# Windowed attention beside a Mish feed-forward on one core: kept rest chunks in a padded layout, one transfer for each rest tile, and another table of places

## The chip, the cores and the metric

The kernel runs on one core of a Trainium2 chip. The metric is the device time of one execution in microseconds (us); lower is better. Three runs of the kernel before took 1120.54, 1127.26 and 1128.27 us, so its median is 1127.26 us.

## What is computed

The input `x` has 2048 rows of 576 columns. Each row is normalised; the result goes through two branches, and both are added to `x`:

```python
xn = (x - mean) / sqrt(var + eps)
# A: 32 heads of 18 columns; a row sees itself and the 7 rows 2, 4, ... 14 before it
q, k, v = split(xn @ wqkv)                       # 576 x 1728
attn = softmax(q . k[pos - 2 * (0..7)] * scale)  # masked where pos - 2 w < 0
A = (attn . v[pos - 2 * (0..7)]) @ wo            # 576 x 576
# B: dense, Mish, dense
h = xn @ w1 + b1                                 # 576 x 4608
B = (h * tanh(softplus(h))) @ w2                 # 4608 x 576
out = x + A + B
```

## The kernel before

**Tiling.** The rows are worked on in two halves (`hf`) of 1024. A product in fp32 is made from numbers split into a high and a low part, so that one tile product costs three matmuls (high x high, high x low, low x high). Most products use a scheme of seven block products for a 2 x 2 block product; the blocks of the weights are called B11, B21, B22 and the sums T1 to T4, those of the activations A11 to A22 and S1 to S4.

**The rest.** The contraction of 576 is four tiles of 128 rows and a rest of 64 rows, 32 for each block row. For the rest, high and low parts are put side by side on the 128 partitions, so that one matmul does the three products of a block. The rest rows of the weights come in as `in_wqr` (for the queries, keys and values) and `in_w1r` (for `w1`). They are prepared in chunks: `c_load` (L1149) brings a chunk in, `c_sum` (L1154, GpSimd) forms the T sums, `c_high` (L1157, ScalarE) and `c_low` (L1161, VectorE) split it, and `c_keep` (L1169) writes it to a tensor in HBM, `ckept`. Chunks "0" and "y" are done whole; "1" to "4" and "v" are done in four pieces of a quarter of their columns each: 32 of 128 columns for "1" to "4", 27 of 108 for "v".

**Reading them back.** `wr_fetch` (L1177) reads the tile `wr` for one step `q` of the feed-forward from `ckept`: 128 partitions of 7 blocks of 128 columns, in two transfers of 64 partitions that read the same rows. `rest_fetch` (L1190) reads the tiles `rest_y`, `rest_v` and `rest_z` for the query, key and value products, also in two transfers each. `wr` has 36 tiles in all, and they share two buffers with some of the rest tiles.

**The order of the work.** The program is a plan of 451 slots. Each slot holds one item of TensorE work (M): a part of a first dense product (`h`, L1388), a group of a second dense product (`po`, L1489, L1579, L1601), a piece of the query, key and value products (`y`, `v`, `z`, L1060) or of the output product (`o`, L1766). All other work is cut into 3316 small functions ("atoms"): loads, splits, evictions, attention steps, stores. The table `PLACES` names for each slot the atoms in their order, and M where its matmuls stand. The instructions of each engine then run in the order in which the atoms were written. `PLACES` thus sets the order on VectorE (DVE), ScalarE (ACT), GpSimd (POOL) and on SyncE (SP), which issues every transfer of the kernel. SP takes its transfers strictly one after the other, and hands them to eight semaphores in turn; a transfer waits until the one before it on its semaphore has landed, until its buffer is free, and until its data are there.

Transfers that the prediction speaks of: `t` (T sums of `w1`: t0, t1), `wa` and `wc` (blocks of `w1`), `wr`, all for the first product; `pw` (blocks of `w2` for the second); `kv` and `q` (attention's inputs); `o_d` (attention's output, stored); `vw_*` and `z_*` (weights of the v and z products); `kv_d`, `q_d` (their results, stored). In a name such as `t1_1_3` the last two numbers are the half and the step `q`. Evictions: L1493 (DVE) adds a `po` result to `acc` and so frees a buffer that a later `po` group writes.

Of the kernel before, what the change touches and what calls it, by code (L numbers as in the profile page):

```python
# [9 lines left out]
F32 = mybir.dt.float32  # L10
# [8 lines left out]
P = 128  # L19
# [14 lines left out]
RB = 32  # L34
CP = 4
QC = UQ * CU * 3 // 4

# [248 lines left out]
PLACES = ("b2 p33 b0 b1 b3 b6 b8 b4 b7 b9 b5 b11 b12 b13 M", "b10 m0a m0b b14 b16 b7a b15 M",  # L286
# [222 lines left out]
def block_kernel(ctx: ExitStack, tc: tile.TileContext, x, wq, wqd, wqr, wo, w1, w1r, b1, w2, mask, sign, out):  # L509
# [620 lines left out]
    def c_tiles(c):  # L1130
        return 7, QC if c[0] in "yv" else P, 64 if c[0] == "4" else P

# [30 lines left out]
    def c_keep(c):  # L1163
        lo, hi, cols = chunk[c]
        n, w, rows = c_tiles(c)
        if c[0] not in ckept:
            ckept[c[0]] = dram.tile([2, rows, n, w], F32, name=f"ckept_{c[0]}")
        for h, t in ((0, hi.bitcast(F32)), (1, lo)):
            nc.sync.dma_start(ckept[c[0]][h][:, :, cols], t)  # L1169
# [1214 lines left out]
```

## Time and profile before

| | |
|---|---|
| time of the profiled execution | 1120.96 us |
| its span, first to last instruction | 1119.2 us |
| mean granted TensorE clock | 0.991 |
| TensorE busy | 1089.2 us, 97% of the span |
| VectorE / ScalarE / GpSimd busy | 899.0 / 522.0 / 801.3 us |
| moved by DMA | 297.15 MB in 241954 packets, 266 GB/s over the span |

The page of the profile gives such sums for one execution. TensorE (PE) is busy nearly all the time, so what matters is where it is not: the timeline of PE gives, in brackets behind a row, how long PE sat idle before that row and what ended the wait. The view by stretches gives busy time of each engine, the granted clock of TensorE (PEclk, 1.00 is full speed), the mean share of the 16 DMA engines that were busy, and the rate in GB/s, for any stretch of the span. The timeline of SP (SPq) shows when each transfer was issued; a long row there means that issues were held up. The list of transfers gives for each kind the count, KB each and the median time from issue to landing.

### The profile page before, as it was taken

The page shows a single profiled execution, that of the slowest core. Times are in us where ns is not written, and L with a number is a line of the kernel's source. Part 1 is how long each engine was busy: PE and PEld are TensorE (multiplying, and loading weights), DVE is VectorE, ACT ScalarE, POOL GpSimd, SP SyncE. Part 2 cuts the span into 40 slices and gives each one's busy share as a digit, 9 for nine tenths or more (in the row PEclk, how much of TensorE's full clock was granted, in tenths as well). Part 3 has the DMA queues.
Part 4 walks back from the last instruction along what each step waited for, and adds up shares of the span by engine and source line. Part 5 has one row for each costly group of instructions (what it writes and reads, how often), then busy time and mean ns, then how long its engine had stood idle before and what let it go on. Part 6 is the DMA issues. An engine that isn't in the chain of part 4 may idle for free.

```text
span 1119.2 us, 18531 instructions
## 1 busy us (share of the span) xinstructions
PE 1089.2 (97%) x6420; PEld 998.4 (89%) x6420; DVE 899.0 (80%) x1520; ACT 522.0 (47%) x994; POOL 801.3 (72%) x709
## 2 busy tenths in 40 slices
PE   8999999999999999989998999999999999999998
PEld 8889899999998898879988878999999898999998
DVE  6897887897888889868996475888788786678886
ACT  7655553654554444547622253524344424343353
POOL 3474888796877688957897488687777687968532
PEclk9999999999999999999999998999999999999999
DMA  7899999879888789996999999678687768697864
GB/s 265 275 292 313 343 307 297 269 247 318 291 258 266 215 251 313 273 279 197 296 337 286 303 291 332 219 251 277 218 257 230 222 198 249 179 316 246 299 185 163
DMA packets 241954, 297.15 MB, mean 266 GB/s; under 512 B 101666, under 2 KB 177860, under 8 KB 241860
## 3 DMA queue, kind: packets, MB, share of 16 engines
q1 hardware_dynamic: 241860, 295.96, 84.9%
q8 instruction: 51, 0.84, 0.3%
q14 instruction: 43, 0.35, 0.1%
HBM read 180.51 MB, written 115.38 MB: 264 GB/s over the span
## 4 chain that ended last, share of the span: by engine, by line
PE 72%; DMA 9%; DVE 6%; POOL 3%; issue 2%; SPq 2%; ACT 1%; DVEq 0%; POOLq 0%; ACTq 0%
PE h L1388 29%; PE po L1489 17%; PE po L1579 11%; PE po L1601 6%; PE o L1766 5%; DMA wr<-ckept 2%; PE v L1060 1%; DMA rw<-in_w 1%; POOL pr L1244 1%; POOL pv L1283 1%; DVE L L1249 1%; DVE acc L1493 1%; DMA vw_B<-kept_wq 1%; DMA z_T<-kept_yT 1%; DMA vw_T<-kept_vT 1%
## 5 line engine op out<-in xcount | busy, mean ns | idle before, releaser
L1489 PE MATMUL po<-w,act 128*128 128x288 f32 x1728 | 244.1, 297 | 3.7 <-DVE acc L1493 3.3
L1489 PEld LDWEIGHTS po<-w,act 128*128 128x128 f32 x1728 | 237.7, 189 | 11.2 <-DVE acc L1493 5.2
L1283 POOL TENSOR_TENSOR pv<-L,kv 128x576 f32<-128x576 f32 x128 | 172.7, 1457 | 56.8 <-DVE L L1276 24.2
L1244 POOL TENSOR_TENSOR pr<-q,kv 128x576 f32<-128x576 f32 x128 | 193.0, 1538 | 9.4 <-DVE og L1289 3.7
L1493 DVE TENSOR_TENSOR acc<-po,acc 128x288 f32<-128x288 f32 x288 | 119.9, 446 | 33.3 <-PE po L1489 32.8
L1579 PEld LDWEIGHTS po<-pw,u 128*128 128x128 f32 x1008 | 139.3, 190 | 4.7 <-issue 0.7
L1579 PE MATMUL po<-pw,u 128*128 128x288 f32 x1008 | 141.9, 297 | 0.1
L1441 POOL TENSOR_TENSOR act<-c,act 128x512 fp32r<-128x512 f32 x66 | 89.7, 1366 | 57.7 <-ACT act L1440 56.5
L1388 PE MATMUL h<-xt,t 128*128 128x512 f32 x432 | 112.4, 395 | 4.1 <-DMA t<-kept_t 2.9
L1388 PE MATMUL h<-xt,wa 128*128 128x512 f32 x432 | 112.1, 396 | 0.0
L1388 PE MATMUL h<-S,t 128*128 128x512 f32 x432 | 110.7, 391 | 0.5 <-ACT ra L1418 0.5
L1388 PE MATMUL h<-xt,wr 128*128 128x512 f32 x252 | 99.3, 394 | 5.3 <-DMA wr<-ckept 5.3
L1289 DVE TENSOR_REDUCE og<-pv 128x144 f32<-128x1152 f32 x64 | 85.9, 1346 | 21.4 <-POOL pv L1283 21.3
L1388 PEld LDWEIGHTS h<-xt,wa 128*128 128x128 f32 x432 | 82.6, 192 | 17.1
L1388 PEld LDWEIGHTS h<-xt,t 128*128 128x128 f32 x432 | 79.7, 190 | 20.1 <-DMA t<-kept_t 3.2
L1249 DVE TENSOR_REDUCE L<-pr 128x64 f32<-128x1152 f32 x64 | 85.6, 1343 | 13.1 <-POOL pr L1244 13.1
L1418 ACT COPY c<-h 128x512 f32<-128x512 f32 x68 | 39.7, 584 | 115.1 <-PE h L1388 115.0
L1585 DVE TENSOR_TENSOR accP<-po,accP 128x288 f32<-128x288 f32 x156 | 64.6, 447 | 33.1 <-PE po L1579 31.1
L1388 PEld LDWEIGHTS h<-S,t 128*128 128x128 f32 x432 | 77.9, 188 | 14.3 <-ACT ra L1418 1.0
L1432 ACT ACTIVATE c<-c,cb 128x512 f32<-128x512 f32 x69 | 49.9, 724 | 65.6 <-DVE c L1429 65.6
L1601 PEld LDWEIGHTS po<-w,act 128*128 128x128 f32 x576 | 78.4, 188 | 2.2 <-DVE accP L1604 0.7
L1601 PE MATMUL po<-w,act 128*128 128x288 f32 x576 | 79.8, 295 | 0.4 <-DVE accP L1604 0.4
(324 smaller groups left out, 2106.1 us busy)
## 6 DMA issues: line engine op xcount, KB each, us to landing
kv<-kv_d SPq DMA_DIRECT2D x64, 396.0 KB, 5.9
kept_t<-t SPq DMA_DIRECT2D x36, 512.0 KB, 5.1
t<-kept_t SPq DMA_DIRECT2D x36, 512.0 KB, 4.5
wr<-ckept SPq DMA_DIRECT2D x72, 224.0 KB, 5.0
pw<-kept_T SPq DMA_DIRECT2D x24, 576.0 KB, 6.0
rw<-in_w SPq DMA_DIRECT2D x36, 288.0 KB, 4.8
kept_B<-w SPq DMA_DIRECT2D x36, 288.0 KB, 3.7
pw<-kept_B SPq DMA_DIRECT2D x18, 576.0 KB, 6.6
```

The source lines that it names most:

```text
L1244: nc.gpsimd.tensor_tensor(out=pr[:, x:x + hh], in0=q[:, j0 + x:j0 + x + hh, None, :].to_broadcast([P, hh, W, CU]), in1=win(kt, 0, CU, j0 + ...
L1249: nc.vector.tensor_reduce(L[:, k, j0:j0 + hj].rearrange("p j w h -> p (j w h)"), pr.rearrange("p j w (h d) -> p (j w h) d", h=2), axis=AX, ...
L1283: nc.gpsimd.tensor_tensor(out=pr[:, x:x + hj].rearrange("p j d w -> p j w d"), in0=L[:, k, x:x + hj, :, h:h + 1].to_broadcast([P, hj, W, DH]),
L1289: nc.vector.tensor_reduce(og[:, c0:c0 + DH, :].rearrange("p d j -> p j d"), pr, axis=AX, op=ALU.add)
L1388: nc.tensor.matmul(ph, l, r_, start=first and i == 0, stop=i == len(seq) - 1, skip_group_check=True)
L1441: inline(lambda: eng.tensor_tensor(out=a[:, 1, :], in0=t, in1=a[:, 0, :].bitcast(F32), op=ALU.subtract))
L1489: nc.tensor.matmul(po, acts[hf, q, b, j][:, al, tok], done["w2", hf, 2 * q + j][:, wl, c * HC:(c + 1) * HC], start=i == 0, stop=i == 5)
L1493: inline(lambda t=t, po=po: nc.vector.tensor_tensor(out=t, in0=po, in1=t, op=ALU.add))
L1579: nc.tensor.matmul(po, units[e, k, qq][:, al, tok], w[:, qq, wl, :], start=i == 0, stop=i == 5)
L1585: inline(lambda t=t, po=po: nc.vector.tensor_tensor(out=t, in0=po, in1=t, op=ALU.add))
L1601: nc.tensor.matmul(po, acts[hf, q, b, j][:, al, tok], done["w2", hf, 2 * q + j][:, wl, c * HC:(c + 1) * HC], start=i == 0, stop=i == 5)
L1766: nc.tensor.matmul(h, l, r_, start=first and n == 0, stop=n == len(seq) - 1, skip_group_check=True)
```

## The change

Three things are changed. First, the chunks "y" and "v" are padded from 108 to 112 columns (also on the host, in `in_wqr`), and the pieces of "v" are now 32, 32, 32 and 16 columns wide. Secondly, `ckept` holds the high and the low part of a row side by side (`[rows, 2, n, w]` in place of `[2, rows, n, w]`), so that the 64 rows of a `wr` tile stand one behind the other, and the tile comes in one transfer of 128 partitions whose source is those 64 rows taken twice: 36 transfers of 448 KB for 72 of 224 KB. Thirdly, the table `PLACES` is another one. It holds the same atoms in the same 451 slots; 978 of the 3316 stand in the same slot, most others some slots earlier or later. The items of TensorE, and the tables that choose buffers and steps, are the same. TensorE keeps its 6420 matmuls in the same order; the transfers go from 965 to 929.

```diff
+QP = 112
...
-    "m3a m3f m3b 18 m3h 14 m3c m3e M", "m4b m4d 19 p34 m4a m3g 22 p35 1 15 m4c m4e 12 25 m4f m4g 23 M",
+    "11 m2h m3a m1i m3b m2i m2k m3c m3f 18 22 m3e m3h M", "m4b m4d m4a p38 p39 19 m4c m4e m4g m4f m4h m4i 23 15 M",
...
     def c_tiles(c):
-        return 7, QC if c[0] in "yv" else P, 64 if c[0] == "4" else P
+        return 7, QP if c[0] in "yv" else P, 64 if c[0] == "4" else P
...
-            w = w // 4
-            cols = slice(int(c[1]) * w, (int(c[1]) + 1) * w)
+            cols = slice(int(c[1]) * 32, min(int(c[1]) * 32 + 32, w))
+            w = cols.stop - cols.start
...
-            ckept[c[0]] = dram.tile([2, rows, n, w], F32, name=f"ckept_{c[0]}")
+            ckept[c[0]] = dram.tile([rows, 2, n, w], F32, name=f"ckept_{c[0]}")
         for h, t in ((0, hi.bitcast(F32)), (1, lo)):
-            nc.sync.dma_start(ckept[c[0]][h][:, :, cols], t)
+            nc.sync.dma_start(ckept[c[0]][:, h, :, cols], t)
...
     def wr_fetch(hf, q):
-        src = ckept[str(w // CP)][:, r0:r0 + RB].rearrange("h r n w -> r h (n w)")
-        for k in range(2):
-            nc.sync.dma_start(t[k * 64:(k + 1) * 64].rearrange("p n w -> p (n w)").bitcast(F32), src)
+        src = ckept[str(w // CP)][r0, 0, 0, 0:1]
+        nc.sync.dma_start(t.rearrange("p n w -> p (n w)").bitcast(F32),
+                          bass.AP(tensor=src.tensor, offset=src.offset, ap=[[0, 2], [7 * P, 2 * RB], [1, 7 * P]]))
...
-        t = sb.tile([P, CP, m, QC], F32R, tag=tag, bufs=bufs, name=f"rest_{which}{n}")
-        src = ckept[c][:, :, ops_[0]:ops_[-1] + 1].rearrange("h (k r) n w -> r h k (n w)", k=CP)
+        t = sb.tile([P, CP, m, QP], F32R, tag=tag, bufs=bufs, name=f"rest_{which}{n}")
+        src = ckept[c][:, :, ops_[0]:ops_[-1] + 1].rearrange("(k r) h n w -> (r h) k (n w)", k=CP)
...
-            rcols[which, CORDER[o]] = t[:, :, k]
+            rcols[which, CORDER[o]] = t[:, :, k, 0:QC]
```

The table's effect is best seen on SP at three places. In the rows, the last number of a name is a counter without meaning, and x4 means four like rows.

The first place is on SP, in the second half at step 2 of the feed-forward, where the tile `t1_1_3` is fetched. Before:

```order
L1201 DMA kv1_1_0_7836<-kv_d0_130 128x792
L1547 DMA pw_0_1_7853<-kept2_T2_0_1749 128x1152
L1201 DMA kv1_1_1_7871<-kv_d0_130 128x792
L1318 DMA o_d0_138<-oT_0_7_7844 32x18x32 x4
L1318 DMA o_d0_138<-oT_0_7_7844 32x16x32 x4
L1201 DMA kv0_1_2_7934<-kv_d0_130 128x792
L1210 DMA q_1_2_7936<-q_d0_134 128x288
L874 DMA t1_1_3_7944<-kept_t1_3_2061 128x1024
```

and with the change:

```order
L1549 DMA pw_0_1_7811<-kept2_T2_0_1747 128x1152
L1563 DMA accP3_0_7369<-in_x 128x2x288
L876 DMA t1_1_3_7822<-kept_t1_3_2334 128x1024
L1563 DMA accP4_1_7366<-in_x 128x2x288
L1203 DMA kv1_1_0_7853<-kv_d0_130 128x792
L962 DMA kv_d3_133<-kvs_z10_7616 128x8x144
L967 DMA q_d3_137<-qs_z10_7615 128x4x144
L1203 DMA kv1_1_1_7898<-kv_d0_130 128x792
```

`t1_1_3` moves ahead of the eight stores `o_d0<-oT_0_7`, which now stand 37 rows behind it, and ahead of four attention loads.

The second place is on SP as well, in the second half at steps 12 and 13, where `wr_1_13` is fetched. Before:

```order
L874 DMA t0_1_14_10314<-kept_t0_14_5348 128x1024
L874 DMA w2_1_27_10382<-kept_w2_27_5526 128x1152
L1547 DMA pw_5_2_10384<-kept_B11_5_4582 128x1152
L1547 DMA pw_5_3_10390<-kept2_T3_5_4784 128x1152
L1547 DMA pw_5_4_10395<-kept_B21_5_4618 128x1152
L1547 DMA pw_5_5_10397<-kept2_T2_5_4779 128x1152
L874 DMA wa_1_14_10487<-kept_wa_14_5434 128x1024
L1201 DMA kv1_1_10_10499<-kv_d2_132 128x792
L1177 DMA wr_1_13_10610<-ckept_3_3478 64x1x896 x2
```

and with the change:

```order
L1178 DMA wr_1_13_10277<-ckept_3_3523 128x1x896
L876 DMA w2_1_26_10310<-kept_w2_26_5414 128x1152
L876 DMA w2_1_27_10312<-kept_w2_27_5778 128x1152
L1320 DMA o_d1_139<-oT_1_3_10124 32x18x32 x4
L876 DMA t0_1_14_10370<-kept_t0_14_5333 128x1024
L876 DMA wc_1_13_10375<-kept_wc_13_5246 128x512
L1549 DMA pw_5_2_10377<-kept_B11_5_4684 128x1152
L1549 DMA pw_5_3_10379<-kept2_T3_5_4755 128x1152
L1549 DMA pw_5_4_10381<-kept_B21_5_4719 128x1152
L1549 DMA pw_5_5_10383<-kept2_T2_5_4855 128x1152
```

`wr_1_13` now stands ahead of the four `pw_5` fetches in place of behind them, and is one transfer.

The third place is on SP between the halves, in the v products, where `rest_v2` is fetched. Before:

```order
L1190 DMA rest_v3_6994<-ckept_v_5359 64x4x108 x2
L1111 DMA z_B11_1_0_6997<-kept_yB11_1_859 128x432
L1111 DMA z_B11_1_1_6998<-kept_yB11_1_859 128x432
L1111 DMA z_B21_0_0_7046<-kept_yB21_0_962 128x432
L1111 DMA z_B21_0_1_7047<-kept_yB21_0_962 128x432
L1190 DMA rest_v2_7051<-ckept_v_5359 64x4x108 x2
```

and with the change:

```order
L1113 DMA z_B11_1_0_6927<-kept_yB11_1_875 128x432
L1113 DMA z_B11_1_1_6928<-kept_yB11_1_875 128x432
L1116 DMA z_T3_0_6932<-kept_yT3_0_1089 128x2x432
L1192 DMA rest_v3_6942<-ckept_v_5353 64x4x112 x2
L1113 DMA z_B21_0_0_6989<-kept_yB21_0_955 128x432
L1113 DMA z_B21_0_1_6990<-kept_yB21_0_955 128x432
L1113 DMA z_B21_1_0_6997<-kept_yB21_1_950 128x432
L1113 DMA z_B21_1_1_6998<-kept_yB21_1_950 128x432
L1192 DMA rest_v2_7016<-ckept_v_5353 64x4x112 x2
```

Here three transfers, `z_T3_0`, `z_B21_1_0` and `z_B21_1_1`, have come in ahead of `rest_v2`.

More of the change, by code (lines that the diff above doesn't have):

```diff
@@ L285 @@
 }
-PLACES = ("b2 p33 b0 b1 b3 b6 b8 b4 b7 b9 b5 b11 b12 b13 M", "b10 m0a m0b b14 b16 b7a b15 M",
[200 rows of a table removed]
+PLACES = ("b2 b0 b1 b3 21 b6 b8 b9 b10 b4 b7 M", "25 0 b5 b11 b13 b14 b12 m0a m0b b16 b15 M",
[201 rows of a table added]
 STEPS = ((27, 28, 30, 32, 35, 42, 46, 50, 57, 59, 62, 68, 73, 78, 81, 87, 91, 96, 100, 108, 111, 114, 121, 126, 130, 135, 140, 144, 148, 155, 158, 162, 166, 169, 170, 173, 179, 180, 186, 189, 192, 196, 198, 200, 201, 205, 208, 214, 218, 227, 228, 229, 230, 232, 233, 234, 235, 237, 238, 239, 240, 241, 242, 243, 244, 245, 246, 247, 248, 250, 251, 252, 253), (257, 258, 259, 260, 261, 264, 268, 269, 272, 275, 277, 279, 281, 284, 288, 289, 291, 294, 295, 298, 301, 303, 305, 307, 310, 313, 315, 317, 319, 322, 324, 325, 329, 331, 333, 335, 338, 341, 343, 345, 348, 351, 354, 355, 358, 360, 363, 367, 370, 372, 375, 379, 383, 385, 387, 389, 391, 394, 396, 398, 400, 402, 404, 406, 408, 410, 412, 414, 416, 418, 420, 422, 423))
@@ L2353 @@
     rp = rests.reshape(2, 2, 2, RB, CP, QC).transpose(0, 2, 1, 4, 3, 5)
-    wqrp = np.ascontiguousarray(blocks(rp).transpose(0, 2, 3, 1, 4).reshape(2, P, 4, QC))
+    wqrp = np.pad(blocks(rp).transpose(0, 2, 3, 1, 4).reshape(2, P, 4, QC), ((0, 0), (0, 0), (0, 0), (0, QP - QC)))
     wop = np.ascontiguousarray(dup(np.asarray(inputs["A_wo"])))
```

399 rows, old and new, of the table PLACES are left out of this document.

## The prediction

> **What bounds the kernel now.** I read the busy times first, then the timeline of TensorE for its idle gaps, then the granted clock behind each gap, and last what SP was doing before each.
>
> ```profile
> PE 1089.2 (97%) x6420; PEld 998.4 (89%) x6420; DVE 899.0 (80%) x1520; ACT 522.0 (47%) x994; POOL 801.3 (72%) x709
> ```
>
> TensorE has work for 97% of the span, in an order that the change leaves alone. So only its 30 us of idle time and a lowered clock can be won. The gaps behind the start-up that are over 1 us, apart from two for VectorE (1.50 at 80 us and 1.06 at 348 us) that I leave as they are, have the bracket at the row's end as their length and cause:
>
> ```profile
> 371.86 4.19 PE L1489 MATMUL po<-w,act 128*128 128x288 f32 x18 [2.20 <-DVE acc L1493]
> 485.54 0.77 PE L1388 MATMUL h<-xt,wr 128*128 128x512 f32 x1 [3.37 <-DMA wr<-ckept]
> 588.02 0.85 PE L1060 MATMUL v<-vw_B,S 128*128 128x432 f32 x3 [1.55 <-DMA vw_B<-kept_wq]
> 607.88 1.45 PE L1060 MATMUL z<-z_T,S 128*128 128x432 f32 x3 [3.17 <-DMA z_T<-kept_yT]
> 645.59 1.62 PE L1388 MATMUL h<-S,wc 128*128 128x512 f32 x6 [1.04 <-DMA wc<-kept_wc]
> 673.75 2.92 PE L1388 MATMUL h<-xt,t 128*128 128x512 f32 x6 [2.92 <-DMA t<-kept_t]
> 925.25 0.67 PE L1388 MATMUL h<-xt,wr 128*128 128x512 f32 x1 [1.90 <-DMA wr<-ckept]
> ```
>
> Six of the seven are transfers that landed late. Each of the five longest costs twice, as the granted clock (PEclk) of the stretch behind it shows; the columns are the stretch, its length, busy times with counts, PEclk, the share of busy DMA engines and GB/s:
>
> ```profile
> 372.00:380.00 8.00, 8.00 (x45) 7.72 (x46) 6.94 (x13) 2.69 (x4) 4.29 (x3) 0.79 0.82 195
> 476.00:486.00 10.00, 6.63 (x39) 5.80 (x38) 6.17 (x10) 1.69 (x3) 5.17 (x4) 0.95 1.07 166
> 486.00:494.00 8.00, 8.00 (x41) 7.01 (x41) 4.50 (x9) 3.75 (x7) 2.21 (x3) 0.85 0.92 304
> 608.00:616.00 8.00, 8.00 (x34) 7.52 (x35) 5.20 (x6) 1.97 (x6) 6.33 (x5) 0.79 1.13 291
> 674.00:682.00 8.00, 8.00 (x34) 7.21 (x35) 3.10 (x6) 0.00 (x0) 5.63 (x5) 0.65 1.08 325
> 926.00:934.00 8.00, 7.99 (x40) 6.51 (x40) 4.00 (x10) 3.39 (x6) 5.42 (x5) 0.83 1.05 318
> ```
>
> Behind the gaps TensorE is busy throughout, so what the clock lacks is lost: 8 x 0.21 = 1.68 us at 372, 8 x 0.15 = 1.20 at 486, 1.68 at 608, 2.80 at 674 and 1.36 at 926. The Trainium skill (TensorE: Matmul & The Clock Gate, Part 1: The HAM clock gate) lets the clock fall to half after an idle window of about 3.4 us. By that, gaps of 1.90 to 3.37 us need have cost no clock, and without the clock parts my sum would come out near 1116 us; here the measurement decides, since a gap of 1.90 us was followed by 0.83, and that case gets no chance of its own.
>
> **The late transfers.** What held them up is seen on SP (start, length, issue):
>
> ```profile
> 474.75 1.29 SPq L1169 DMA_DIRECT2D ckept_v<-ck_v  x2
> 476.14 1.59 SPq L1177 DMA_DIRECT2D wr<-ckept  x2
> 594.97 5.07 SPq L1318 DMA_DIRECT2D o_d<-oT  x4
> 603.54 1.07 SPq L1111 DMA_DIRECT2D z_T<-kept_yT  x2
> 657.61 9.47 SPq L1318 DMA_DIRECT2D o_d<-oT  x8
> 668.21 0.38 SPq L874 DMA_DIRECT2D t<-kept_t  x1
> 908.66 0.32 SPq L1547 DMA_DIRECT2D pw<-kept_B  x1
> 913.74 0.32 SPq L1547 DMA_DIRECT2D pw<-kept_T  x1
> 915.65 1.15 SPq L1177 DMA_DIRECT2D wr<-ckept  x2
> ```
>
> The tile `t1_1_3` was wanted at 670.83 (673.75 less 2.92) and issued at 668.21, behind eight stores that took 9.47 us to issue and that nothing wants soon. With the change it stands ahead of them. `wr_1_13` was issued at 915.65, behind `pw` fetches that wait 5 us each for their buffers; now it stands ahead of all four. `z_T2_1` was behind four such stores and three attention loads and now stands ahead of them. `wr_0_16` was behind the keeps of a "v" chunk, in a stretch where the DMA engines are full at only 166 GB/s; now it stands ahead of those keeps. `wc_1_1` stands ahead of `wr_1_1` in place of behind it. I take these five gaps as gone: 3.37 + 3.17 + 1.04 + 2.92 + 1.90 = 12.40 us, and the clock behind four of them, 1.20 + 1.68 + 2.80 + 1.36 = 7.04; together **-19.4 us** (bounds 0 and -19.4). The `vw_B` tile at 588.02 passes only a few neighbours in a full stretch; I leave its 1.55 us.
>
> **The gap at 371.86** came from an eviction that stood behind one odd VectorE instruction:
>
> ```profile
> 365.67 5.17 DVE L1161 TENSOR_TENSOR ck<-ck 64x224 fp32r<-64x224 f32 x1
> L1161 DVE TENSOR_TENSOR ck<-ck x17: 373/501/5169, 31.2 to 403.7; 128x224 fp32r<-128x224 f32 x12, 64x224 fp32r<-64x224 f32 x4, 128x896 fp32r<-128x896 f32 x1
> 365.78 2.81 POOL L1244 TENSOR_TENSOR pr<-q,kv 128x576 f32<-128x576 f32 x2
> ```
>
> Its like take 0.37 to 0.50 us (min and median); this one took 5.17 while GpSimd ran an unbroken chain beside it. In the new table it stands a whole item earlier, ahead of all evictions of that item, but whether it meets such a chain again is chance. I take half of 2.20 + 1.68: **-1.9 us** (bounds 0 and -3.9).
>
> **The packing.** These rows price it (count, KB each, median us to landing):
>
> ```profile
> t<-kept_t SPq DMA_DIRECT2D x36, 512.0 KB, 4.5
> wr<-ckept SPq DMA_DIRECT2D x72, 224.0 KB, 5.0
> wa<-kept_wa SPq DMA_DIRECT2D x18, 512.0 KB, 5.9
> ckept<-ck SPq DMA_DIRECT2D x24, 112.0 KB, 4.7
> ckept_v<-ck_v SPq DMA_DIRECT2D x8, 94.5 KB, 6.9
> rest_v<-ckept_v SPq DMA_DIRECT2D x6, 108.0 KB, 4.0
> L1169 SPq DMA_DIRECT2D ckept_v<-ck_v x8: 513/544/830, 428.7 to 507.0; - x8
> L1190 SPq DMA_DIRECT2D rest_v<-ckept_v x10: 579/592/1042, 525.0 to 567.8; - x10
> L1154 POOL TENSOR_TENSOR ck_v<-ck_v x16: 233/242/691, 418.6 to 496.4; 128x27 f32<-128x27 f32 x16
> ```
>
> The trace has no `wr` of 448 KB. The nearest rows, 512 KB in 4.5 or 5.9 us, are the bounds; a pair lands some 0.6 us (half of 1.15) + 5.0 = 5.6 us after its first issue. So a tile lands between 1.1 us sooner and 0.3 us later. TensorE waits for `wr` at two places only, both counted above: **0** (-2.2 to +0.6). 36 issues of some 0.6 us leave SP, which wins nothing where SP waits for a buffer; that is in the 0. The "v" pieces of 32 columns should land like the `ckept` pieces, which are already 32 wide: 4.7 for 6.9 us. Their cover is that the last is issued at 507.0 and the first reader at 525.0; without it, the 2.2 us would count. Four padded columns in 108 make the 16 sums on GpSimd, of 242 ns each, some 4% longer, 0.14 us in all, and the like on ScalarE and VectorE, all beside TensorE's work: 0.
>
> **What the new order makes late.** At `rest_v2` three transfers, 432 + 216 + 216 = 864 KB, have come in ahead:
>
> ```profile
> 567.17 1.24 SPq L1190 DMA_DIRECT2D rest_v<-ckept_v  x2
> 575.74 0.36 PE L1060 MATMUL vT<-rest_v,xt 128*128 128x432 f32 x1
> 556.00:580.00 24.00, 23.62 (x120) 22.27 (x120) 22.35 (x31) 10.86 (x30) 19.86 (x17) 1.00 1.07 347
> z_T<-kept_yT SPq DMA_DIRECT2D x4, 432.0 KB, 8.5
> ```
>
> Before, its second half was out at 568.41 and landed some 4.0 us later, 3.3 us ahead of its use at 575.74. The DMA engines are full here, so 864 KB at 347 GB/s take 2.5 us of that: 0.8 us are left, and no gap. But that half is the eighth transfer behind `z_T3_0` and so must wait for it on its semaphore: issued at some 566.1 and landed 8.5 us later, that is 574.6; plus 4.0 is 578.6, or 2.9 us late, with a clock part of 1.7 as at 608. Between 0 and +4.6 us I take the middle, **+2.3**.
>
> Two thirds of all atoms have moved, and I can't follow each. The bounds are 0 and as much as the seven gaps cost now with their clock: 12.40 + 7.04 + 3.88 + 1.55 = 24.9 us. The new rows at the five places all put what TensorE needs next ahead of stores, so I go near the lower end: two gaps like that at 925.25 (1.90 + 1.36 each), **+6.5 us**.
>
> **The sum** goes against the profiled execution's own 1120.96 us: 1120.96 - 19.4 - 1.9 + 2.3 + 6.5 = 1108.4. That execution lies 6.3 us below the median of the three runs shown (1127.26). I read the spread as one or two late transfers more, and since the changed order leaves more room for these, I add half of it: about **1111.5 us**.
>
> **Rivals.**
>
> *The full stretch stays as it is.* From 556 to 646 us the DMA engines are busy throughout (shares 1.05 to 1.13 above), so what moves ahead makes something else late by the same bytes. Then only the gaps at 485, 673 and 925 go: 1120.96 - (3.37 + 1.20 + 2.92 + 2.80 + 1.90 + 1.36) + 4.6 + 6.5 = 1118.5, and half the spread above that, 1121.6. For it speaks that `rest_v2` did get later; against it that the stores and attention loads that were passed are not wanted there.
>
> *The gaps only change their places.* As many transfers come late as before: 1120.96 + 3.1 = 1124. For it: SP still waits for buffers in order,
>
> ```profile
> SPq L874 <- PE h L1388: 90.9, 18, 12.3
> ```
>
> so a fetch put too early holds up all behind it. Against it: the five rows above were put right singly.
>
> *Every gap goes, and no new one comes:* 1120.96 - 24.9 + 3.1 = 1099.
>
> *Slower: VectorE starves at the evictions.* An instruction like that at 365.67 in front of an eviction costs 3.9 us. VectorE's order has changed nearly everywhere, so its instructions meet GpSimd's chains at other places. From nine such hits on (1120.96 - 19.4 + 3.1 + 9 x 3.9 = 1139.8) the kernel is slower by over 1%; ten give about 1144. Against it: the trace has one hit in 1119 us.
>
> **Chances.** A measurement of this kernel can tell about 1% (11 us) from no change. The forecast (1104 to 1118) has 0.49; the full stretch 0.24; changed places 0.11; all gone 0.08; slower 0.08. Faster by over 1% means under 1116.0: 0.46 of the forecast and 0.08 make 0.54. Within 1%: 0.03 + 0.24 + 0.11 = 0.38. Slower: 0.08. The range runs from 1101 (the forecast with no new gap, -6.5 and -2.3, and the one at 371.86 wholly gone, -1.9) to 1126, so that it holds the full stretch and the changed places.
>
> **What would show it.** Right: no idle time of PE for `wr`, `t` and `z_T` near 485, 608, 674 and 925, PEclk 1.00 there, PE's idle time below 20 us, a mean clock above 0.991; `wr` x36 at 448 KB landing in 4.5 to 5.9 us; a gap of up to 2.9 us at `rest_v2`. Wrong: gaps of over 1.5 us at other tiles with as much in sum, or VectorE instructions of over 3 us in front of `po` groups.

## The result and the profile after

The changed kernel takes **1270.82 us** (median of four runs, 1266.62 to 1275.25) against 1126.75 (1120.54 to 1128.27): a ratio of 1.129, 95% interval 1.123 to 1.135. It is 13% slower. The forecast was 1111.5 us, and no rival came near it.

The page of the profile of the changed kernel, its execution of 1266.62 us (span 1264.8): busy times, the clock of TensorE in 40 slices, and the queue that SP fills:

```profile
PE 1121.8 (89%) x6420; PEld 1018.7 (81%) x6420; DVE 885.8 (70%) x1520; ACT 519.8 (41%) x993; POOL 785.6 (62%) x709
PEclk9998998999998998998999898899899988999999
q1 hardware_dynamic: 240780, 296.20, 74.4%
```

TensorE now idles 1264.8 - 1121.8 = 143.0 us where it was 30.0, and is busy 32.6 us longer for the same 6420 matmuls, at a mean clock of 0.958 in place of 0.991 (1089.2 x 0.991 / 0.958 would be 1126.7, so the clock is reason enough). Line numbers of the kernels differ by a few from those of before. VectorE, ScalarE and GpSimd have not become slower: their busy times are 2 to 16 us below those of before. The DMA engines are less busy too, and yet transfers are what everyone waits for. From the view of waits (who waited for whom; us in total, times, longest):

```profile
PE po L1491 <- POOL act L1443: 22.2, 8, 9.1
PE po L1581 <- DMA pw<-kept_B: 21.2, 4, 7.0
PE h L1390 <- DMA wr<-ckept: 17.9, 7, 5.6
PE po L1581 <- DMA pw<-kept_T: 10.3, 2, 9.9
PE h L1390 <- DMA wc<-kept_wc: 8.9, 2, 7.4
PE h L1390 <- DMA wa<-kept_wa: 7.0, 3, 4.9
PE h L1390 <- DMA t<-kept_t: 6.9, 3, 3.7
```

```profile
POOL tt L831 <- DMA rw<-in_w: 35.1, 5, 13.3
POOL pv L1285 <- DMA kv<-kv_d: 28.3, 3, 12.6
```

The first row is not GpSimd's own slowness: its waits for `rw` and `kv`, in the second fence, were 17.3 and 6.1 us before, and a GpSimd that waits for loads comes late with `act`; in the run wr_two below, this row is gone. The lost time is spread over loads of every kind, and `wr` itself is only 17.9 us of it. So something holds up the loads together. One place shows how. SP's timeline of the changed kernel (start, length of the issue or issues, line, transfer):

```profile
888.85 2.07 SPq L1178 DMA_DIRECT2D wr<-ckept  x1
890.97 0.52 SPq L876 DMA_DIRECT2D wc<-kept_wc  x1
891.59 0.38 SPq L1203 DMA_DIRECT2D kv<-kv_d  x1
892.01 0.46 SPq L1212 DMA_DIRECT2D q<-q_d  x1
892.51 0.44 SPq L1549 DMA_DIRECT2D pw<-kept_T  x1
892.99 2.36 SPq L1549 DMA_DIRECT2D pw<-kept_B  x1
895.39 3.57 SPq L1549 DMA_DIRECT2D pw<-kept_T  x2
915.54 0.32 SPq L1549 DMA_DIRECT2D pw<-kept_B  x1
```

The list of transfers gives no landing times for this kernel. I took them from the trace, from the times at which each transfer's semaphore was raised (the last raise of each counts):

| transfer | issued | landed | after |
|---|---|---|---|
| `wr_1_8`, one transfer of 448 KB | 888.9 | 906.0 | 17.2 |
| `wc_1_8` | 891.0 | 906.7 | 15.7 |
| `kv0_1_7` | 891.6 | 907.6 | 16.1 |
| `q_1_7` | 892.0 | 908.0 | 16.0 |
| `pw_2_5` | 892.5 | 909.4 | 16.9 |
| `pw_2_6` | 893.0 | 910.8 | 17.9 |
| `pw_3_0` | 895.4 | 912.3 | 16.9 |
| `pw_3_1` | 898.1 | 913.7 | 15.6 |

Seven transfers come after `wr_1_8`, and all land behind it, one after another, 0.4 to 1.4 us apart, though they go to other tiles. The semaphore of such a transfer is raised 16 times: for `wc_1_8` fourteen times by 893.9 us, and the last two times at 906.4 and 906.7. That holds over the whole run: of the 227 transfers issued while a `wr` was in flight, the fourteenth raise came 4.8 us after issue and the sixteenth 12.9 us (medians). SP issued nothing between 898.96 and 915.54: the buffer for the next `pw` came free when the `po` group that had waited was done, at 909.56 + 5.95 = 915.51. So a late landing also makes the next issue late. What the DMA engines did meanwhile is in the view by stretches of the changed kernel (columns as in the prediction: DMA share and GB/s stand last), and in TensorE's timeline:

```profile
891.00:904.00 13.00, 8.69 (x49) 7.41 (x47) 7.76 (x12) 4.64 (x8) 10.10 (x8) 1.00 0.92 245
904.00:909.00 5.00, 0.00 (x0) 0.00 (x0) 0.00 (x0) 0.00 (x0) 0.00 (x0) 0.60 0.13 51
```

```profile
899.30 0.39 PE L1390 MATMUL h<-xt,wr 128*128 128x512 f32 x1
909.56 5.95 PE L1581 MATMUL po<-pw,u 128*128 128x288 f32 x24 [9.87 <-DMA pw<-kept_T]
```

From 904 to 909 us the share of busy DMA engines is 0.13, which is 2 of 16, while all compute engines stand still. Read together with the two late raises: fourteen engines have nothing left to do, and two still work off what these transfers left with them. The trace's packets say the same over the whole run. A `wr` tile is 128 packets of 3584 B. In the kernel before, some 9.0 packets of that size were in flight at once while any was; in the changed kernel 2.07, and two at a time for 341 of the 384 us in which there were up to three. At 0.165 us each (mean), 128 packets two at a time take 10.6 us. `wr` tiles land 14.1 us after issue (median; 12.1 to 19.0) where each half landed after 5.7 (the list of transfers, which gives 5.0 there, follows only some of the semaphores, so its medians differ a little from mine). Other transfers issued while a `wr` was in flight land after 12.9 us, against 5.0 for those that were not (medians); before, it was 6.1 and 5.1.

Here the Trainium skill has the rule (DMA: Bandwidth & Descriptors, Rules for kernel authors): "an outermost dim of size c < 16 — e.g. a leading zero-stride broadcast of c copies — confines the whole DMA to at most c engines". The new source is `[[0, 2], [7 * P, 64], [1, 7 * P]]`, so c is 2, and the 2.07 packets at once and the share of 0.13 agree.

### The profile page after: what moved, and what is told of

The parts are those of the page before. It is cut to its first block, busy times and chain, and to the rows that moved or that the text cites. A ratio compares the mean times of both kernels' runs of the same rounds, so it can differ in the third digit from the quotient of the medians.

```text
span 1264.8 us, 18465 instructions
## 1 busy us (share of the span) xinstructions
PE 1121.8 (89%) x6420; PEld 1018.7 (81%) x6420; DVE 885.8 (70%) x1520; ACT 519.8 (41%) x993; POOL 785.6 (62%) x709
## 4 chain that ended last, share of the span: by engine, by line
PE 28%; DMA 15%; SPq 3%; DVE 2%; POOL 2%; issue 1%; ACT 0%; DVEq 0%; ACTq 0%; POOLq 0%
PE h L1390 8%; PE po L1581 6%; DMA pw<-kept_B 5%; PE o L1768 4%; PE po L1603 4%; DMA pw<-kept_T 2%; DMA wa<-kept_wa 2%; DMA t<-kept_t 2%; DMA kv_d<-kvs_z 1%; PE v L1062 1%; PE z L1062 1%; DMA wc<-kept_wc 1%; DMA accP<-in_x 1%; POOL pv L1285 1%; SPq L1320 1%; SPq L876 1%
## 5 line engine op out<-in xcount | busy, mean ns | idle before, releaser
L1491 PE MATMUL po<-w,act 128*128 128x288 f32 x1728 | 251.5, 301 | 35.7 <-POOL act L1443 22.2
L1491 PEld LDWEIGHTS po<-w,act 128*128 128x128 f32 x1728 | 242.6, 193 | 46.6 <-POOL act L1443 24.0
L1581 PE MATMUL po<-pw,u 128*128 128x288 f32 x1008 | 151.6, 309 | 32.3 <-DMA pw<-kept_B 21.2
L1581 PEld LDWEIGHTS po<-pw,u 128*128 128x128 f32 x1008 | 148.3, 202 | 37.9 <-issue 21.2
L1390 PE MATMUL h<-xt,wa 128*128 128x512 f32 x432 | 118.5, 413 | 14.9 <-ACT wa L848 7.9
L1390 PE MATMUL h<-xt,wr 128*128 128x512 f32 x252 | 101.1, 401 | 17.9 <-DMA wr<-ckept 17.9
L1390 PEld LDWEIGHTS h<-xt,wa 128*128 128x128 f32 x432 | 86.5, 201 | 34.9 <-ACT wa L848 8.3
L1603 PE MATMUL po<-w,act 128*128 128x288 f32 x576 | 80.6, 296 | 2.3 <-issue 1.4
L1603 PEld LDWEIGHTS po<-w,act 128*128 128x128 f32 x576 | 78.4, 188 | 5.2 <-issue 1.8
L1390 PEld LDWEIGHTS h<-xt,wr 128*128 128x128 f32 x252 | 48.6, 193 | 31.3 <-DMA wr<-ckept 21.1
```

Source lines behind the costliest of these rows:

```text
L1390: nc.tensor.matmul(ph, l, r_, start=first and i == 0, stop=i == len(seq) - 1, skip_group_check=True)
L1491: nc.tensor.matmul(po, acts[hf, q, b, j][:, al, tok], done["w2", hf, 2 * q + j][:, wl, c * HC:(c + 1) * HC], start=i == 0, stop=i == 5)
L1581: nc.tensor.matmul(po, units[e, k, qq][:, al, tok], w[:, qq, wl, :], start=i == 0, stop=i == 5)
L1603: nc.tensor.matmul(po, acts[hf, q, b, j][:, al, tok], done["w2", hf, 2 * q + j][:, wl, c * HC:(c + 1) * HC], start=i == 0, stop=i == 5)
```

## The experiments

**Theory F** (few engines): the leading dimension of 2 puts each `wr` on two DMA engines for over 10 us, and everything behind it on these two lands late. **Rivals:** T, the new table issues loads too late or too early; L, rows side by side read worse; S, a transfer of 448 KB lands late in any form; R, reading the same rows twice in one transfer is what is slow. Ratios are to runs of the kernel before on the same chip.

### Which part of the change costs

**wr_two**: the change with `wr` in two transfers again.

```diff
-        nc.sync.dma_start(t.rearrange("p n w -> p (n w)").bitcast(F32),
-                          bass.AP(..., ap=[[0, 2], [7 * P, 2 * RB], [1, 7 * P]]))
+        for k in range(2):
+            nc.sync.dma_start(t[k * 64:(k + 1) * 64].rearrange("p n w -> p (n w)").bitcast(F32),
+                              bass.AP(..., ap=[[7 * P, 2 * RB], [1, 7 * P]]))
```

> The changed kernel with one thing undone: each wr tile comes in two transfers of 64 rows again, from the new side-by-side layout, under the new table. Theory F (few DMA engines): the one wr transfer, whose source has a leading dimension of 2, moves two packets at a time, so it takes 14.2 us to land where a half took 5.8, and everything behind it on those engines lands late too. Then this kernel's wr lands in 5 to 6 us, no other kind of transfer has landings over 11 us, and the time is 1100 to 1126 us, near the 1111.5 predicted. Rival T (the table): the new order issues fetches so that they are late on this chip; then the time stays above 1240 us. Rival L (the layout): rows side by side read worse; then wr lands in 10 us or more and the time is above 1200.

Measured: **1097.25 us**, ratio 0.975 (0.970 to 0.980), 3 us under the expected bounds. The whole loss was in those lines: 1270.8 - 1097.3 = 173.6 us, 4.8 us for each of 36 tiles. It is also faster than the forecast and than both kernels. The longest landing of any other transfer issued beside a `wr` is 10.5 us. Its page, and its waits of TensorE:

```profile
PE 1080.3 (99%) x6420; PEld 994.0 (91%) x6420; DVE 889.6 (81%) x1520; ACT 519.2 (47%) x993; POOL 800.0 (73%) x709
q1 hardware_dynamic: 241860, 296.21, 85.7%
wr<-ckept SPq DMA_DIRECT2D x72, 224.0 KB, 4.9
```

```profile
PE po L1582 <- DVE accP L1588: 2.4, 2, 1.9
PE v L1062 <- DVE acc L1496: 2.0, 1, 2.0
PE z L1062 <- DMA z_B<-kept_yB: 0.3, 1, 0.3
```

The same bytes as in the changed kernel keep the engines busy for 85.7% of a span that is 168.6 us shorter.

**one_old_table**: the change with the table of before in place of the new one.

> The table of places of before, with everything else of the change: padded chunks, rows side by side, one transfer for a wr tile. Theory F: wr lands in 12 to 19 us as in the changed kernel, and the time is 1220 to 1300 us. Rival T (the table is what costs): 1118 to 1130 us.

Measured: 1309.33 us, ratio 1.161 (1.157 to 1.166), 9 us over the expected bounds. With the old table the loss is there as well, so rival T falls. The single transfer costs 188.7 us under the old table (1309.3 for the 1120.6 of layout_only, next) and 173.6 under the new one.

**layout_only**: the table of before, new layout, `wr` in two transfers.

> The table of places of before and the new layout, with each wr tile in two transfers of 64 rows: what padding, 32-wide parts and side-by-side rows do alone. Theory F, and the prediction's packing term of 0 (-2.2 to +0.6 us): 1118 to 1128 us, within 1% of before. Rival L (the layout is what costs): above 1200 us.

Measured: 1120.60 us, ratio 0.994 (0.992 to 0.997). Rival L falls.

**table_only**: the kernel before with the new table alone.

> The kernel before with the new table of places alone: old chunks of 108 columns, old layout, wr in two transfers. If the table's gain needs nothing else of the change: 1095 to 1110 us, some 0 to 7 us above the run with two transfers and the new layout (1097), as the new layout alone took 6 us off the old table. If the table only fits the padded pieces (rival): over 1115.

Measured: 1103.19 us, ratio 0.979 (0.973 to 0.985). The new table brings 22.4 us without the rest of the change.

### Why the single transfer is slow

**whole**: one transfer of 448 KB from 128 successive rows.

```diff
-        src = ckept[str(w // CP)][r0, 0, 0, 0:1]
+        src = ckept[c][min(r0, 0 if c == "4" else 2 * RB), 0, 0, 0:1]
...
-        bass.AP(..., ap=[[0, 2], [7 * P, 2 * RB], [1, 7 * P]])
+        bass.AP(..., ap=[[7 * P, P], [1, 7 * P]])
```

> The changed kernel, with one transfer of 448 KB for a wr tile, but its source one run of 128 successive rows instead of the same 64 rows twice: rows 64 to 127 of wr are then other rows of the kept block than the reference needs (and the block's start is moved where it would run past its end), so the output is not the reference's. Theory F: as the leading dimension is no longer 2, all 16 engines take part, wr lands in 4.5 to 6 us and the time is 1100 to 1126. Rival S (size: a transfer of 448 KB lands late in whatever form): wr lands in 12 to 14 us as in the changed kernel and the time is 1250 to 1280. Rival T (table): wr lands early, the time stays above 1240.

Measured: 1099.17 us, ratio 0.974 (0.969 to 0.978), 1 us under the expected bounds. From its list of transfers (count, KB each, median us to landing):

```profile
wr<-ckept SPq DMA_DIRECT2D x36, 448.0 KB, 5.2
```

A transfer of 448 KB lands in 5.2 us, so rival S falls.

**inner_repeat**: the same 64 rows read twice, with the repetition as the second dimension.

```diff
-        bass.AP(..., ap=[[0, 2], [7 * P, 2 * RB], [1, 7 * P]])
+        bass.AP(..., ap=[[7 * P, 2 * RB], [0, 2], [1, 7 * P]])
```

> The changed kernel, one transfer for a wr tile, the same 64 rows each read twice, but with the repetition as the second dimension: the source's leading dimension is 64, and each row goes to two partitions beside each other (so most partitions hold another row than the reference needs). Theory F: all 16 engines take part, wr lands in 4.5 to 6 us and the time is 1093 to 1106. Rival R (reading rows twice in one transfer costs): over 1150 us.

Measured: 1096.50 us, ratio 0.973 (0.970 to 0.977).

```profile
wr<-ckept SPq DMA_DIRECT2D x36, 448.0 KB, 4.9
```

The same rows, the same double reading, the same size; only the order of two dimensions differs, and 174 us are gone. Rival R falls.

**lead2, lead4, lead8**: 2, 4 or 8 pieces that overlap by one row, so that no dimension can be joined with the next. The start of the block is moved as in whole.

```diff
-        bass.AP(..., ap=[[0, 2], [7 * P, 2 * RB], [1, 7 * P]])
+        bass.AP(..., ap=[[63 * 7 * P, 2], [7 * P, 64], [1, 7 * P]])   # lead4: 31, 4, 32; lead8: 15, 8, 16
```

> The changed kernel with one transfer for a wr tile whose source again has a leading dimension of 2, but of two pieces 63 rows apart, so that no rows are read twice but one: rows 63 to 127 of wr are then other rows than the reference needs. Theory F (the leading dimension sets how many of the 16 engines take part): two packets at a time, wr lands in 12 to 15 us, 1250 to 1290 us. Rival R (reading the same 64 rows twice in one transfer is what was slow): wr lands in 4.5 to 6 us and the time is 1093 to 1106.

> As the one with two pieces, with four pieces of 32 rows, 31 rows apart (most rows of wr are then other rows than the reference needs). Theory F: four packets at a time, so 128 packets of 0.17 to 0.21 us take 5.4 to 6.7 us, and wr lands in 7 to 9 us; the time lies between, 1105 to 1160. Rival R: as the one of one run of rows, 4.5 to 6 us and 1093 to 1106.

> The same with eight pieces of 16 rows, 15 rows apart (most rows of wr are then other rows than the reference needs). Theory F: eight packets at a time, 2.7 to 3.4 us of packets, wr lands in 5 to 7 us; the time is 1093 to 1115. Rival R: 4.5 to 6 us and 1093 to 1106. A rival of a threshold (anything under 16 pieces goes to two engines) has wr at 12 us or more and 1250 or more.

Measured, with the landings and packets from the traces of each run (packets of 3584 B in flight while any was; medians of landing, us):

| leading dimension | kernel | packets at once | `wr` lands | others beside it | time, us | ratio (95%) |
|---|---|---|---|---|---|---|
| 2 (step 0) | the change | 2.07 | 14.1 | 12.9 | 1270.82 | 1.129 (1.123 to 1.135) |
| 2 | lead2 | 2.06 | 14.4 | 12.8 | 1271.18 | 1.128 (1.121 to 1.135) |
| 4 | lead4 | 3.69 | 11.1 | 9.9 | 1162.99 | 1.032 (1.025 to 1.039) |
| 8 | lead8 | 6.52 | 7.9 | 7.3 | 1109.05 | 0.984 (0.979 to 0.990) |
| 64 | inner_repeat | 9.03 | 5.1 | 5.5 | 1096.50 | 0.973 (0.970 to 0.977) |
| 128 | whole | 8.93 | 5.3 | 5.6 | 1099.17 | 0.974 (0.969 to 0.978) |
| 64, two transfers | wr_two | 9.27 | 5.0 | 5.5 | 1097.25 | 0.975 (0.970 to 0.980) |

The packets at once follow the leading dimension, and the landing of the neighbours follows that of `wr`. (With 64 or 128 the number rises to 18 within a transfer and falls again, so its mean is 9.) The step of 0 plays no part. The results for 4 and 8 pieces lie between those for 2 and 64, so the rival of a threshold falls as well. Twice I set the landing too low, 7 to 9 us for four pieces (11.1) and 5 to 7 for eight (7.9), by counting only the transfer's own packets; other transfers' packets in the same queues are the likely rest, which no run separates. The time of four pieces came out 3 us over its bounds. The traces agree with the Trainium skill's way of choosing the number of engines as well (DMA: Bandwidth & Descriptors, Why a DMA increments its semaphore by 16 and not by 1: the largest number up to 16 that divides the slowest dimension of both sides).

**half_tiles**: the single transfer for the 18 tiles of the first half, two transfers for the second half's.

```diff
+        for k in range(2) if hf else ():
+            nc.sync.dma_start(t[k * 64:(k + 1) * 64]...)
+        if hf == 0:
+            nc.sync.dma_start(t...)   # ap=[[0, 2], ...]
```

> The changed kernel with the wr tiles of the first half (18 of 36) in one transfer with a leading dimension of 2, those of the second half in two transfers. Theory F with a price for each tile: half of the 174 us between 1097 and 1271 us, so 1165 to 1205; PE gaps over 3 us lie up to the end of the first half's wr fetches alone. If the loss comes from one place of the program (a rival), all of it or none: under 1110 or over 1255.

Measured: 1189.14 us, ratio 1.055 (1.051 to 1.060). That is 91.9 us above wr_two, or 5.1 for each tile. The stretches of its first and second half:

```profile
86.00:600.00 514.00, 444.43 (x2484) 396.01 (x2483) 347.64 (x593) 216.00 (x381) 314.50 (x343) 0.94 0.73 233
600.00:1188.00 588.00, 579.20 (x3503) 536.08 (x3501) 467.85 (x787) 248.62 (x469) 430.96 (x319) 1.00 0.83 262
```

TensorE idles 514.00 - 444.43 = 69.6 us in the first stretch at a clock of 0.94, and 8.8 in the second at 1.00. The loss goes with the tiles, so it has no single place.

### Which part of the packing brought 6 us

**pad_only**: the kernel before with chunks of 112 columns in parts of 32, and nothing else. **side_only**: the kernel before with high and low rows side by side, and nothing else.

> The kernel before with the padding alone: chunks of 112 columns, in parts of 32; table, layout and two transfers as before. Padding and side-by-side rows together took 6 us off (1120.6 for 1126.9). If the parts of 32 columns bring it, as they land sooner (the prediction's bound for them was 2.2 us): 1119 to 1123 us. If the rows side by side bring it: 1124 to 1129. For both, fewer small packets for the padded chunks.

> The kernel before with the side-by-side rows alone: chunks of 108 columns, the table and two transfers of 64 successive rows. If reading 64 successive rows is what brings the 6 us: 1119 to 1123 us; if the padding brings it: 1124 to 1129.

Measured: pad_only 1119.12 us, ratio 0.994 (0.992 to 0.997); side_only 1125.80, ratio 1.000 (0.998 to 1.002). All of it is the padding (6.5 us, by the interval 4 to 9). The single traces can't divide these us up: the traced execution of pad_only took 1123.52 us, more than the traced one of before. They show what is gone at one place. TensorE's timeline of side_only still has the wait at 485 us that the prediction began with:

```profile
485.43 0.77 PE L1389 MATMUL h<-xt,wr 128*128 128x512 f32 x1 [4.06 <-DMA wr<-ckept]
```

With the padding alone, under the old table, it is gone (stretch of pad_only, and its keeps of "v"):

```profile
476.00:486.00 10.00, 10.00 (x60) 8.98 (x59) 8.04 (x14) 3.85 (x7) 8.35 (x6) 1.00 0.91 260
```

```profile
ckept_v<-ck_v SPq DMA_DIRECT2D x6, 112.0 KB, 5.8
ckept_v<-ck_v SPq DMA_DIRECT2D x2, 56.0 KB, 4.4
```

`wr_0_16` was issued at 477.1 us in the kernel before and at 478.3 with the padding (its second half); it landed 8.3 us after that in the one and 4.2 in the other. The two keeps just ahead of it landed after 7.3 and 8.9 us, and with the padding after 3.0 and 3.4.

## Why the prediction was wrong

**The step that failed** is the packing: "The trace has no `wr` of 448 KB. The nearest rows, 512 KB in 4.5 or 5.9 us, are the bounds", and from it "**0** (-2.2 to +0.6)". It chose the nearest rows by their bytes. Apart from five small ones at the start (16 KB or less), every transfer of the kernel before has a leading dimension of 32 or more, so none of its rows is near in the quantity that decided. The term is +174 us (1270.8 for 1097.3), and its two parts are a `wr` that lands in 14.1 us for 5.7, and, the larger one, all that queues behind it on the same two engines (17.9 us of TensorE's waits in the changed kernel are for `wr`, 54.3 for the other transfers listed). The prediction gave the single transfer a price only where TensorE waits for `wr`; whoever is issued behind it was not in the sum. The rule quoted above was not among its rivals. As a mechanism of this kernel it would have stood there with a price from rows: 128 packets on 2 engines in place of 16. The same term also held the padding at 0, with 2.2 us as its most; the padding brought 6.5.

**The five late transfers, -19.4: right.** With two transfers per tile, PE has no wait of over 0.3 us for any transfer left, and the clock is full in the stretches of the span where it was 0.95, 0.85, 0.79 and 0.65 (stretches of wr_two; the work in them is some us further on than before):

```profile
476.00:486.00 10.00, 10.00 (x68) 9.43 (x67) 8.26 (x18) 3.98 (x6) 7.73 (x11) 1.00 1.04 345
486.00:494.00 8.00, 8.00 (x53) 7.33 (x53) 6.27 (x12) 5.69 (x11) 4.13 (x9) 1.00 0.92 290
608.00:616.00 8.00, 7.70 (x39) 7.07 (x39) 7.29 (x17) 0.42 (x1) 3.69 (x3) 1.00 1.07 350
674.00:682.00 8.00, 8.00 (x56) 7.65 (x55) 7.08 (x11) 2.79 (x7) 5.73 (x4) 1.00 1.03 335
```

TensorE's idle time is 15.9 us (below the 20 named) for 30.0, and it is busy 8.9 us less, which is mostly the clock (0.997 for 0.991): together 23.0 us of the span. In the other traces with the new table and a `wr` that is spread over the engines (table_only, whole, inner_repeat), TensorE waits for transfers 0.4 to 1.3 us in all. One of the five has two sufficient causes: the wait at 485 us goes with the table alone, and with the padding alone as well.

**The gap at 371.86: chance, as the prediction said.** With the new table it is small in one trace and larger than before in another. Here are wr_two and table_only:

```profile
360.56 3.45 PE L1492 MATMUL po<-w,act 128*128 128x288 f32 x24 [0.79 <-DVE acc L1496]
365.15 4.98 PE L1490 MATMUL po<-w,act 128*128 128x288 f32 x24 [3.13 <-DVE acc L1494]
```

The `ck` instruction on VectorE in front took 2.15 us in wr_two and 4.24 in table_only, for 5.17 before; inner_repeat has a gap of 0.79 us, whole one of 2.95. To take half was thus a fair price. That GpSimd caused the long ones stays unproven.

**The new order's own losses: +2.3 did not come, +6.5 did, at another place.** PE waits for no `rest_v` tile in wr_two, and its waits for transfers are 0.3 us in all. But two gaps of about 2 us are new in its trace, both wait for VectorE, and the clock is lowered behind both:

```profile
542.69 2.53 PE L1062 MATMUL v<-vw_B,xt 128*128 128x432 f32 x6 [2.01 <-DVE acc L1496]
814.52 3.80 PE L1582 MATMUL po<-pw,u 128*128 128x288 f32 x18 [1.95 <-DVE accP L1588]
543.00:551.00 8.00, 8.00 (x35) 7.54 (x35) 6.69 (x10) 4.54 (x11) 6.74 (x5) 0.81 0.54 164
815.00:823.00 8.00, 8.00 (x46) 7.58 (x45) 6.97 (x12) 0.62 (x1) 4.61 (x4) 0.79 0.46 153
```

With the clock, that is 2.01 + 1.52 + 1.95 + 1.68 = 7.2 us, near the 6.5 by luck, since neither the place nor the cause was foreseen. The first gap belongs to the new order: table_only, whole and inner_repeat have it too, with 1.98 or 1.99 us. The second stands in this trace alone, behind a VectorE instruction of 5.43 us (L1525). That is one hit of the kind that the last rival, a VectorE starved by GpSimd, counted on.

**"Costs twice" is not a fixed price.** The prediction read a lowered clock behind each of the five longest gaps. The gap before `v` is followed by a clock of 0.79 in wr_two and table_only (8 us from the end of the gap), and by 1.00 in whole and inner_repeat, though it is as long. So the clock parts held for the execution that was read, not for gaps of that length in general.

**The lower end.** Without the single transfer, the time (1097.25) lies below the range's lower end of 1101 and near that of the rival in which every gap goes (1099). That rival's mechanism did not come true, since new gaps came. What made up for them is, in part, that gaps went which the prediction had left as they were (1.55, 1.50 and 1.06 us), and the padding. What was added for the spread of the runs (+3.1) did not come either.

**VectorE starved by GpSimd** was the only rival on the slower side. In the changed kernel VectorE's busy time fell to 885.8 us, and the loss goes with the lines of `wr` alone, so it is not the mechanism of the slowdown.

**The sum as measured:** table -22.4, padding -6.5, rows side by side 0, single transfer +174; from 1126.8 that gives 1271.9 against 1270.8.

## What to carry to other kernels

Before joining two transfers into one, look at the leading dimension of the new source and destination, not at the bytes: a repetition belongs in an inner dimension, or in two transfers. A transfer that runs on few DMA engines has a price for everything that is issued behind it, so look for landings that come one after another behind one transfer, and for a DMA share near a small number of sixteenths while the compute engines stand still. Here joining had nothing to win even when it was spread well (1096.5 and 1099.2 against 1097.25 with two transfers): with two transfers TensorE waits for transfers only 0.3 us in all, so SP's issue time was not what it waited for.

## What was not expected of the hardware

The runs of 108 B that the kernel before writes to HBM slow down what moves beside them. In the kernel before, the "v" keeps write them; in the stretch around one pair of them (449 to 460 us) the packets of 4096 B of the other transfers took 653 ns on the mean, against 185 over the run, while the 108 B packets themselves took 15. With the padding the runs are 128 B, as many (1792 in that stretch), and the packets of 4096 B take 180 ns. The stretch that holds most of it, of the kernel before and of pad_only:

```profile
450.00:458.00 8.00, 8.00 (x46) 7.02 (x45) 8.00 (x13) 5.23 (x10) 7.41 (x7) 1.00 1.05 136
```

```profile
450.00:458.00 8.00, 8.00 (x57) 7.68 (x56) 8.00 (x15) 4.59 (x9) 5.38 (x5) 1.00 0.96 312
```

The engines are full in both, at 136 and at 312 GB/s. Length alone is not what matters: the last piece of a padded "v" is written in 1792 runs of 64 B, shorter still, and beside them the packets of 1728 B and more took 49 ns per KB in wr_two, with the engines full (DMA share 1.01), against 48 over the run. Beside the runs of 108 B it was 64 to 115 ns per KB wherever the engines were full (before, side_only, table_only). A padded run begins at a multiple of 64 B in its tensor (rows of 448 B), most runs of 108 B do not (rows of 432 B). That fits a cost of where a run begins, but no run changes this alone.
